# Attention tiles of a transformer block: x loads and h stores on SyncE's queue instead of GpSimd's, and one tile of h transposed by TensorE instead of by DMA

## The chip, the core and the metric

The kernel runs on one core of a Trainium2 chip, in one launch. The metric is the device time in microseconds. The engines are called as in the profile: PE is TensorE (matmuls; PEld its weight loads), DVE is VectorE, ACT is ScalarE, POOL is GpSimd, and SP is SyncE, which computes nothing and issues DMAs. A DMA issued by any of them runs on the core's DMA engines; POOL's go through one queue and SP's through another.

## The reference

Linear attention on a layer-normed x, added to x, and then a gated feed-forward part on the layer-normed sum h. There are 2048 tokens of width 1024, 32 heads of width 32, and F = 3584; all is bfloat16.

```python
def _A_ref(x, wqkv, wo):
    # q, k, v: split of x @ wqkv into 32 heads
    phi = lambda t: jnp.where(t > 0, t + 1, jnp.exp(t)) + 1e-6
    pq, pk = phi(q), phi(k)
    kv = einsum("bhsd,bhse->bhde", pk, v)
    z = einsum("bhsd->bhd", pk)
    num = einsum("bhqd,bhde->bhqe", pq, kv)
    den = einsum("bhqd,bhd->bhq", pq, z)[..., None] + 1e-6
    return heads_joined(num / den) @ wo

def _B_ref(x, W_gate, W_up, W_down):
    gate, up = x @ W_gate, x @ W_up
    return (gate * (gate > 0) * up) @ W_down

h  = x + _A_ref(_layernorm(x), A_wqkv, A_wo)
h2 = h + _B_ref(_layernorm(h), B_W_gate, B_W_up, B_W_down)
```

## The kernel before

The 2048 tokens are 16 tiles of 128. The large products are done by a Strassen-like scheme (`strassen`): seven products of half-size blocks in place of eight, for which sums of the left blocks (`left_sums`, L117 to L120, on DVE) and of the weights are formed first. The matmul accumulates in PSUM tiles with the tags A, D and E; tag D has one buffer.

The program goes through four stages in time. Up to about 125 us, k and v are computed and summed over the tokens (the tiles of x are loaded on SP's queue, normalised, and transposed: the first four by PE in `transpose_in`, L283 and L284, the others by a DMA on SP's queue, L274). Then q is computed, first for one half of the tokens and then for the other. From about 150 to 290 us the attention output and h are made tile by tile, mixed with the second half of q and, later, with the first four f-blocks of the gate and up products (`early_quad`, L705). From about 300 us the rest of the gate and up products (L785) follows, and from about 585 us the down product.

The change is in the third stage. `attn_stages(t)` returns five steps for one tile t, and `attn_step(step)` calls them with a lag of 0, 1, 1, 2 and 4 steps, so that up to five tiles are in work. The list `order` holds the tiles in their order in time; below, "tile n" is the n-th of it, 0 to 15. Tiles 0 to 7 are the first half, whose h the first f-blocks need; the last of it is tile 7, `order[STS - 1]`.

- `nd`: the matmuls of numerator and denominator (L511), their logarithm and exponential on ACT (L515, L517), the quotient on DVE into `o_sb` (L518).
- `oT`: a DMA transpose of `o_sb` into `oT` on SP's queue (L525).
- `x_in`: the tile's x is loaded again for the residual, on POOL's queue (L529), into the buffer `x_res`, of which there are three (`XB`).
- `wo_h`: the matmuls with wo (L541); on DVE the residual addition, which also sums h for the mean (L543, in place in `x_res`); the store of h to DRAM, on POOL's queue (L546); the mean on DVE (L551); on ACT the variance (L553), three small steps (L554 to L556) and the normalised h into the buffer `hn` (L557), of which there are two (`HB`).
- `hn_T`: a DMA transpose of `hn` into its columns of `hnT` on SP's queue (L560).

After `hn_T` of the tiles 4 to 7 and 12 to 15, `attn_step` issues the left sums of that tile's columns on DVE.

An x load reuses the buffer of the tile three before it. It therefore waits until that tile's h is stored and until ACT has read it for the last time (L557). The variance step L553 writes into `hn`, and so waits until the transpose of the tile two before it has landed.

Two other kinds of work share the queues of this stage. The gate and up weights of the first groups are loaded on SP's queue (L486), each held back by a one-element copy on POOL (`hold`, L142) that waits for an `o_sb`. The results of `early_quad` are stored on SP's queue (L720).

The order of the instructions on each engine and queue in this stage isn't written out by hand: it is fixed when the program is built, by the readiness and the priority of each instruction, and the instructions of several steps are interleaved. From the stage of L785 on, PE, DVE and ACT follow the program's order. An engine or queue carries out its list in order, and an instruction that waits holds those behind it.

Of the kernel before, what the change touches and what calls it, by code (L numbers as in the profile page):

```python
# [10 lines left out]
BF16 = mybir.dt.bfloat16  # L11
# [20 lines left out]
def block_kernel(ctx: ExitStack, tc: tile.TileContext, x, wqkv, wo, wg, wu, wd, out, H: int):  # L32
    nc = tc.nc
    P = 128
    xf = x.flatten_outer_dims()
    of = out.flatten_outer_dims()
    S, D = xf.shape
# [4 lines left out]
    KC = D // P  # L42
# [5 lines left out]
    KH = KC // 2  # L48
# [9 lines left out]
    ident = consts.tile([P, P], BF16, name="ident")  # L58
# [12 lines left out]
    h_dram = [[dram.tile([P, NT, D], BF16, name=f"h_dram{i}_{s}") for s in range(NS)] for i in range(2)]  # L71
# [133 lines left out]
    order = [(i * HS + s * SW) // P + tt for s in range(NS) for i in range(2) for tt in range(NT)]  # L205
# [5 lines left out]
    pspool = psctx.enter_context(tc.tile_pool(name="ps", bufs=1, space=PSUM))  # L211
    with ExitStack() as actx:
# [208 lines left out]
        for c in range(KC):  # L421
            bnk, i = divmod(c, GPB)
# [41 lines left out]
    hnT, hns = [], []  # L464
# [32 lines left out]
    def attn_stages(t):  # L497

        i, r = divmod(t * P, HS)
        s, r = divmod(r, SW)  # L500
        st = {}

        def nd():
            o_sb = bwork.tile([P, D], BF16, tag="o_sb", name="o_sb")
            st["o"] = o_sb
            held.append(o_sb)
            ov = o_sb[:].rearrange("p (k h e) -> p k h e", k=KC, h=HPC)
            for c0, n in pieces:
                ps = ndpool.tile([P, NW], FP32, tag="ab", name="nd")
                for c in range(c0, c0 + n):  # L510
                    nc.tensor.matmul(ps[:, (c - c0) * NDW:(c - c0 + 1) * NDW], lhsT=pqT[:, c, t * P:(t + 1) * P],  # L511
                                     rhs=kvz[:, c, :], start=True, stop=True)
                ndv = ps[:, 0:n * NDW].rearrange("p (k w) -> p k w", w=NDW)
                den = bsmall.tile([P, GPB, HPC], FP32, tag="den", name="den")
                nc.scalar.activation(out=den[:, 0:n], in_=ndv[:, :, P:NDW], func=ACT.Ln, bias=deps[:], scale=1.0)  # L515
                rd = bsmall.tile([P, GPB, HPC], FP32, tag="rd", name="rd")
                nc.scalar.activation(out=rd[:, 0:n], in_=den[:, 0:n], func=ACT.Exp, scale=-1.0)  # L517
                nc.vector.tensor_tensor(  # L518
                    out=ov[:, c0:c0 + n], in0=ndv[:, :, 0:P].rearrange("p k (h e) -> p k h e", h=HPC),
                    in1=rd[:, 0:n, :].unsqueeze(3).to_broadcast([P, n, HPC, Dh]), op=ALU.mult)  # L520

        def oT():
            oT = bwork.tile([P, D], BF16, tag="oT", bufs=XB, name="oT")
            st["oT"] = oT[:].rearrange("p (c t) -> p c t", c=KC)
            nc.sync.dma_start_transpose(out=st["oT"], in_=st["o"][:])  # L525

        def x_in():
            x_sb = bwork.tile([P, D], BF16, tag="x_res", bufs=XB, name="x_res")
            nc.gpsimd.dma_start(out=x_sb[:], in_=xf[t * P:(t + 1) * P, :])  # L529
            st["x"] = x_sb  # L530

        def wo_h(borrow):
            h_sb = st["x"]
            tot = bsmall.tile([P, 2], FP32, tag="tot", name="tot")
            for j in range(2):
                if borrow:
                    ps = pspool.tile([P, NW], FP32, tag="E", bufs=2, name="attn")
                else:
                    ps = abpool.tile([P, NW], FP32, tag="ab", name="attn")
                for c in range(KC):  # L540
                    nc.tensor.matmul(ps[:], lhsT=st["oT"][:, c, :], rhs=wo_sb[:, c, j * NW:(j + 1) * NW],  # L541
                                     start=(c == 0), stop=(c == KC - 1))
                nc.vector.scalar_tensor_tensor(out=h_sb[:, j * NW:(j + 1) * NW], in0=ps[:], scalar=1.0,  # L543
                                               in1=h_sb[:, j * NW:(j + 1) * NW], op0=ALU.mult, op1=ALU.add,
                                               accum_out=tot[:, j:j + 1])
            nc.gpsimd.dma_start(out=h_dram[i][s][:, r // P, :], in_=h_sb[:])  # L546
            st["hn"] = bwork.tile([P, D], BF16, tag="hn", bufs=HB, name="hn")

            sm = bsmall.tile([P, 6], FP32, tag="sm", name="sm")
            nmean, var, lnv, rstd, nmr = (sm[:, i:i + 1] for i in range(5))  # L550
            nc.vector.tensor_scalar(out=nmean, in0=tot[:, 0:1], scalar1=tot[:, 1:2], scalar2=-1.0 / D,  # L551
                                    op0=ALU.add, op1=ALU.mult)
            nc.scalar.activation(out=st["hn"][:], in_=h_sb[:], func=ACT.Square, bias=nmean, scale=1.0, accum_out=var)  # L553
            nc.scalar.activation(out=lnv, in_=var, func=ACT.Ln, bias=LN_EPS, scale=1.0 / D)  # L554
            nc.scalar.activation(out=rstd, in_=lnv, func=ACT.Exp, scale=-0.5)
            nc.scalar.activation(out=nmr, in_=nmean, func=ACT.Identity, scale=rstd)  # L556
            nc.scalar.activation(out=st["hn"][:], in_=h_sb[:], func=ACT.Identity, bias=nmr, scale=rstd)  # L557

        def hn_T():
            nc.sync.dma_start_transpose(out=hnT[s][i][:, :, r:r + P], in_=st["hn"][:])  # L560

        return nd, oT, x_in, wo_h, hn_T

    LAG = (0, 1, 1, 2, 4)
    STS = ST // NS
# [163 lines left out]
    for f in range(NE):  # L729
        st = {}  # L730
# [149 lines left out]
    for r, (wt, f, fi, toks) in enumerate(runs):  # L880
        w = [ops() for _, ops in now]
        later = []
        for n, s in enumerate(toks):
# [51 lines left out]
            if k == nwin - 3:  # L935
                for x in range(2):
                    t = wpools[1].tile([P, KC * 2 * GP * P], BF16, tag=("wg", "wu")[x], name="wd")
# [16 lines left out]
    for n in range(2):  # L954
        t = fpool.tile([P, 4 * D], BF16, tag="wraw", bufs=2, name="xd")
# [242 lines left out]
    for n in range(1, len(OUTER)):  # L1198
# [73 lines left out]
        else:  # L1272
            pss = []
            for p in range(4):
# [13 lines left out]
                s, t0 = divmod(2 * p, NT)  # L1288
# [55 lines left out]
```

## Time and profile before

| | |
|---|---|
| median of 3 runs | 750.96 us (750.52 to 752.11) |
| the profiled execution | 750.52 us |
| its span | 748.7 us |
| mean granted PE clock | 0.997 |
| PE busy | 723.2 us, 97% |
| DVE, ACT, POOL busy | 563.1, 322.4, 23.1 us |
| POOL's DMA queue | 32 transfers of 256 KB, 8.39 MB |
| DMA engines, mean rate | 176 GB/s |

The span goes from the first to the last instruction of the profiled execution; the time holds 1.8 us more, of what lies around it. Busy times of several engines overlap. Rows of the timeline show the start in us, the duration in us, the engine, the line and the operation with its output and inputs, the number of instructions merged, and in brackets how long the engine had been idle before and what ended that. Rows of the waits show the total in us, how many times, and the longest. Rows of the stretches show the busy time and number of instructions of PE, PEld, DVE, ACT and POOL, then the granted clock, the busy share of the DMA engines, and GB/s. "SPq" is SP's queue.

### The profile page before, as it was taken

To read this page: it belongs to the slowest core of one execution; us is meant where nothing else is said; L and a number is where in the kernel's file an instruction comes from. 1 tells how busy PE (TensorE), PEld (TensorE's weight loads), DVE (VectorE), ACT (ScalarE), POOL (GpSimd) and SP (SyncE) were. 2 spreads that over 40 slices of the span, in tenths; PEclk is the share of its full clock that TensorE was granted. 3 is DMA by queue.
4 is the path that set the end of the run, shared out by engine and by line. 5 is a ranking of instruction groups with operands and counts; after the bars stand their busy time and mean duration, and the time that the engine had idled before them with its cause. 6 is when DMAs were issued, how large, how long until landed. Compare 5 with 4: busy or idle time off the path is not lost.

```text
span 748.7 us, 10599 instructions
## 1 busy us (share of the span) xinstructions
PE 723.2 (97%) x3967; PEld 382.1 (51%) x4020; DVE 563.1 (75%) x991; ACT 322.4 (43%) x580; POOL 23.1 (3%) x76
## 2 busy tenths in 40 slices
PE   7999999999879989999999999999999999999997
PEld 3444555444434434444444444444444458888666
DVE  6997653775867568687787788877787469996797
ACT  4785653878577555444444344443435220000000
POOL 0000000011111000000000000000000000000000
PEclk9999999999999999999999999999999999999999
DMA  9765003079778635154837439466574299887822
GB/s 319 165 135 155 0 1 111 3 172 222 169 161 185 127 85 180 39 171 126 244 116 204 138 132 313 149 213 221 182 260 148 94 389 360 314 288 297 311 73 83
DMA packets 144532, 132.04 MB, mean 176 GB/s; under 512 B 50912, under 2 KB 128096, under 8 KB 144480
## 3 DMA queue, kind: packets, MB, share of 16 engines
q1 hardware_dynamic: 130784, 114.84, 51.4%
q0 software_dynamic: 2560, 8.39, 3.6%
q10 hardware_dynamic: 11136, 8.13, 3.4%
q8 instruction: 31, 0.51, 0.3%
q14 instruction: 21, 0.17, 0.1%
HBM read 79.95 MB, written 39.85 MB: 160 GB/s over the span
## 4 chain that ended last, share of the span: by engine, by line
PE 77%; DVE 8%; ACT 6%; DMA 6%; issue 2%; SPq 0%; DVEq 0%; POOL 0%; ACTq 0%
PE accA L785 22%; PE accX L785 8%; PE accY L785 8%; PE accA L1117 8%; DMA hn<-hn 3%; PE Aq L298 3%; PE accA L946 3%; PE Aq L438 3%; PE attn L541 3%; PE accX L1117 3%; PE accY L1117 2%; PE Eq L298 2%; PE accY L946 2%; PE accX L946 2%; PE Aq L705 1%
## 5 line engine op out<-in xcount | busy, mean ns | idle before, releaser
L795 ACT ACTIVATE gu<-gu 128x512 bf16<-128x512 bf16 x72 | 45.4, 630 | 131.2 <-DVE gu L794 131.2
L790 ACT COPY snap<-accA 128x1024 f32<-128x1024 f32 x72 | 72.5, 1008 | 36.6 <-PE accA L785 36.5
L541 PE MATMUL attn<-wo_mem,oT 128*128 128x512 bf16 x248 | 59.8, 386 | 5.6 <-DVE x_res L543 3.7
L785 PEld LDWEIGHTS <-tg 128*128 128x128 f16 x384 | 37.5, 98 | 45.3
L785 PEld LDWEIGHTS <-tu 128*128 128x128 f16 x384 | 37.5, 98 | 45.4
L794 DVE TENSOR_TENSOR gu<-accY,snap 128x1024 bf16<-128x1024 f32 x36 | 43.9, 1219 | 10.0 <-ACT snap L790 10.0
L785 PE MATMUL accA<-hn,tg 128*128 128x512 f16 (+1 forms) x192 | 49.3, 379 | 0.0
L785 PE MATMUL accA<-hn,tu 128*128 128x512 f16 (+1 forms) x192 | 49.3, 379 | 0.0
L154 ACT COPY u<-Aq 128x512 f32<-128x512 f32 x56 | 32.3, 582 | 38.5 <-PE Aq L298 20.0
L794 DVE TENSOR_TENSOR gu<-accX,snap 128x1024 bf16<-128x1024 f32 x36 | 43.9, 1219 | 6.5 <-PE accX L785 3.7
L1117 PEld LDWEIGHTS <-x 128*128 128x128 f16 (+1 forms) x448 | 43.8, 98 | 5.6
L785 PEld LDWEIGHTS <-wg 128*128 128x128 bf16 x288 | 28.2, 98 | 34.0
L785 PEld LDWEIGHTS <-wu 128*128 128x128 bf16 x288 | 28.1, 98 | 34.0
L541 PEld LDWEIGHTS <-oT 128*128 128x128 bf16 x256 | 24.9, 99 | 35.0 <-issue 4.9
L798 DVE TENSOR_TENSOR hq<-gu 128x512 bf16<-128x512 bf16 x48 | 20.3, 423 | 14.3 <-ACT gu L795 14.2
L298 PEld LDWEIGHTS <-xT 128*128 128x128 bf16 (+1 forms) x192 | 18.6, 98 | 24.4 <-issue 3.0
L1117 PEld LDWEIGHTS <-xs 128*128 128x128 f16 x280 | 27.3, 98 | 3.4
L543 DVE SCALAR_TENSOR_TENSOR x_res<-attn,x_res 128x512 bf16<-128x512 f32 x32 | 21.9, 687 | 8.6 <-PE attn L541 8.6
L946 PEld LDWEIGHTS <-x 128*128 128x128 bf16 (+1 forms) x168 | 16.4, 98 | 19.6
L518 DVE TENSOR_TENSOR o_sb<-nd,rd 128x384 bf16<-128x384 f32 (+1 forms) x48 | 22.6, 506 | 4.4 <-ACT rd L517 4.4
L1123 DVE TENSOR_TENSOR snap<-accA,u 128x1024 f32<-128x1024 f32 x16 | 19.5, 1219 | 8.4 <-PE accA L1117 8.3
L785 PE MATMUL accA<-hs,tg 128*128 128x512 f16 x96 | 24.6, 379 | 0.0
(234 smaller groups left out, 1418.4 us busy)
## 6 DMA issues: line engine op xcount, KB each, us to landing
x<-x_dram SPq DMA_DIRECT2D x17, 896.0 KB, 8.5
x_dram<-hq SPq DMA_DIRECT2D x28, 512.0 KB, 3.3
wg<-in_B_W_gate_dram SPq DMA_DIRECT2D x14, 512.0 KB, 5.4
wu<-in_B_W_up_dram SPq DMA_DIRECT2D x14, 512.0 KB, 7.2
wraw<-in_B_W_down_dram SPq DMA_DIRECT2D x14, 512.0 KB, 4.9
x_dram<-hq SPq DMA_DIRECT2D x28, 256.0 KB, 2.8
t_dram<-wt SPq DMA_DIRECT2D x28, 256.0 KB, 2.2
xd<-x_dram SPq DMA_DIRECT2D x6, 896.0 KB, 7.0
```

The source lines that it names most:

```text
L154: nc.scalar.copy(out=snaps[nm, v], in_=A[v][:])
L298: nc.tensor.matmul(ps[:], lhsT=left[m - 1][:, kc, r + v * P:r + (v + 1) * P], rhs=right[m - 1][:, kc, :], start=(start and kc == 0), stop= ...
L438: nc.tensor.matmul(ps[:], lhsT=rq[m - 1][:, kc, (c + v) * P:(c + v + 1) * P], rhs=left[m - 1][:, kc, :], start=(start and kc == 0), stop=( ...
L518: nc.vector.tensor_tensor(out=ov[:, c0:c0 + n], in0=ndv[:, :, 0:P].rearrange("p k (h e) -> p k h e", h=HPC), in1=rd[:, 0:n, :].unsqueeze(3 ...
L541: nc.tensor.matmul(ps[:], lhsT=st["oT"][:, c, :], rhs=wo_sb[:, c, j * NW:(j + 1) * NW], start=(c == 0), stop=(c == KC - 1))
L543: nc.vector.scalar_tensor_tensor(out=h_sb[:, j * NW:(j + 1) * NW], in0=ps[:], scalar=1.0, in1=h_sb[:, j * NW:(j + 1) * NW], op0=ALU.mult, ...
L785: nc.tensor.matmul(ps[:, v, :], lhsT=w[v][n - 1][:, kc, :], rhs=left[n - 1][:, kc, :], start=(t is not None and kc == 0), stop=(kc == KH - ...
L790: nc.scalar.copy(out=st[nm][:], in_=halves(st["A"]))
L794: add(out=g[:], in0=halves(st[nm]), in1=st[base][:], op=ALU.add)
L795: nc.scalar.activation(out=g[:, 0, :], in_=g[:, 0, :], func=ACT.Relu)
L946: nc.tensor.matmul(ps[:, t * NW:(t + 1) * NW], lhsT=x_tile(n, s, kh)[:, f, (t0 + t) * P:(t0 + t + 1) * P], rhs=w_tile(n, kh)[:, f, :], sta ...
L1117: nc.tensor.matmul(pv[:, tt, :], lhsT=left(m)[:, f, tt * P:(tt + 1) * P], rhs=right(m)[:, f, :], start=(t is not None and f == 0 and tt % ...
```

## The change

In the attention tiles the x load and the h store are issued by SP instead of POOL. For tile 7, `hn_T` no longer issues a DMA transpose: PE transposes the eight blocks of 128 x 128 into one PSUM tile with the tag D, and ACT and DVE each copy one half of it into `hnT`. The left sums of tile 7 then read it from there as before.

```diff
         def x_in():
             x_sb = bwork.tile([P, D], BF16, tag="x_res", bufs=XB, name="x_res")
-            nc.gpsimd.dma_start(out=x_sb[:], in_=xf[t * P:(t + 1) * P, :])
+            nc.sync.dma_start(out=x_sb[:], in_=xf[t * P:(t + 1) * P, :])
...
-            nc.gpsimd.dma_start(out=h_dram[i][s][:, r // P, :], in_=h_sb[:])
+            nc.sync.dma_start(out=h_dram[i][s][:, r // P, :], in_=h_sb[:])
...
         def hn_T():
+            if t == order[STS - 1]:
+                pt = pspool.tile([P, KC, P], BF16, tag="D", bufs=1, name="tp")
+                for kc in range(KC):
+                    nc.tensor.transpose(pt[:, kc, :], st["hn"][:, kc * P:(kc + 1) * P], ident[:])
+                nc.scalar.copy(out=hnT[s][i][:, 0:KH, r:r + P], in_=pt[:, 0:KH])
+                nc.vector.tensor_copy(out=hnT[s][i][:, KH:KC, r:r + P], in_=pt[:, KH:KC])
+                return
             nc.sync.dma_start_transpose(out=hnT[s][i][:, :, r:r + P], in_=st["hn"][:])
```

## The prediction

> **What bounds the kernel now.** I read the page first, then the chain that ended last, then the stretches of time, the waits and the timeline of the stretch that the change touches. The page says that TensorE (PE) is the bound almost everywhere:
>
> ```profile
> span 748.7 us, 10599 instructions
> PE 723.2 (97%) x3967; PEld 382.1 (51%) x4020; DVE 563.1 (75%) x991; ACT 322.4 (43%) x580; POOL 23.1 (3%) x76
> ```
>
> The stretches show where the missing 25 us lie: from 300 to 585 us PE is busy for 283.81 of 285 us, but from 160 to 230 us for 61.02 of 70, from 230 to 260 for 29.30 of 30, and from 260 to 300 for 36.70 of 40. So the attention stretch, 160 to 300 us, holds 13.0 us of idle PE. What comes after is dense, so that a microsecond won or lost here reaches the end. In the chain that ended last, the transposes of h (`DMA hn<-hn`) have 3.4% of the span: five pieces of 6.14, 6.54, 4.43, 5.42 and 3.06 us. The waits of 150 to 300 us say who stands behind them (total, times, longest):
>
> ```profile
> DVE hs L117 <- DMA hn<-hn: 12.9, 6, 3.8
> ACT hn L553 <- DMA hn<-hn: 4.4, 2, 3.4
> PE attn L541 <- DVE x_res L543: 3.7, 1, 3.7
> PE nd L511 <- DVE o_sb L518: 2.0, 1, 2.0
> ```
>
> PE hardly waits for a transpose itself. VectorE (DVE) does, at the first of the left sums (L117), with the residual additions (L543) queued behind, and those release PE's PSUM tiles. The timeline shows the worst case, tile 5:
>
> ```profile
> 210.00 1.23 SPq L560 DMA_TRANSPOSE hn<-hn  x1
> 210.27 0.54 POOL L529 DMA_DIRECT2D x_res<-in_A_x_dram  x1 [2.35 <-ACT hn L557]
> ...
> 212.26 1.26 SPq L525 DMA_TRANSPOSE oT<-o_sb  x1
> ...
> 216.57 0.42 DVE L117 TENSOR_TENSOR hs<-hn 128x512 f16<-128x512 bf16 x1 [3.79 <-DMA hn<-hn]
> 216.65 1.15 ACT L553 ACTIVATE hn<-x_res,sm 128x1024 bf16<-128x1024 bf16 x1 [3.44 <-DMA hn<-hn]
> ...
> 217.67 0.10 PEld L541 LDWEIGHTS <-oT 128*128 128x128 bf16 x1 [2.57 <-DMA oT<-o_sb]
> ...
> 219.00 1.01 PE L541 MATMUL attn<-wo_mem,oT 128*128 128x512 bf16 x2 [3.71 <-DVE x_res L543]
> ```
>
> One transpose takes 6.5 us and stops DVE, ScalarE (ACT) and PE in turn. After it PE even runs at half clock for 3 us (the granted clock is the 0.50; then share and GB/s of the DMAs):
>
> ```profile
> 219.00:222.00 3.00, 3.00 (x11) 1.41 (x11) 3.00 (x10) 2.60 (x8) 1.08 (x2) 0.50 0.54 49
> ```
>
> That is 1.5 us more, so this stall costs 5.2 us.
>
> **Why the transposes are slow.** I asked for the landing time of each h transpose (L560), and compared it with the nearest x load from GpSimd (POOL, L529). With that load issued between 1.7 us before and 0.9 us after it (tiles 0, 1, 2, 4 to 8, 10, 11, 12) a transpose landed in 6.0, 6.1, 6.0, 5.5, 6.5, 5.6, 4.4, 5.0, 4.5, 4.4 and 5.4 us: median 5.5. Without it (tiles 3, 9, 13, 14, 15) it took 3.1 or 3.3. The pairing is no accident: the load waits for its buffer until the second normalising pass (L557) of the tile three back, which is what releases that tile's transpose. Before 40 us the same 256 KB loads go out on SyncE's (SP's) queue, 0.8 to 1.7 us ahead of a transpose of the same shape (xT), and that one still lands in 3.0 to 3.4 us, once in 4.3. Beside the POOL loads of 40.2 and 49.5 us it takes 4.7 and 6.2.
>
> **Part 1, x loads and h stores from POOL to SP.** POOL loses 32 issues of 0.54 us, none of which anyone waits for. SP gains 32; its own x loads show 0.53 us each, 17 us in all, 29 of them after 160 us. SP is idle for about half of the stretch, so only those that fall in front of a ready transpose count. Load and transpose become ready together, and the load stands first in the program. Load first: the transpose is issued 0.5 us later and has 256 KB ahead of it. A 512 KB weight load issued 0.6 us ahead of an oT transpose (159.2 us) made that one 4.8 us instead of 3.1, so half the bytes cost about 0.85. Sum 0.5 + 0.85 + 3.1 = 4.45 us against the median of 5.5: 1.1 us gained. Transpose first: 3.2 us, 2.3 gained. And if SP's load stretches it as POOL's did, 0.5 lost. I take 1.1, since the rows before 40 us speak against the last.
>
> The Trainium skill, "DMA: Bandwidth & Descriptors", section "Issuing engines are not separate DMA queues", speaks against this: whoever issues, all transfers share the same 16 engines, and spreading them only saves the issuer's time. By it alone the transposes stay as slow, SP's 0.5 us stands in front of each, and the sum of this part is a loss of 1 to 2 us; the split of 5.5 against 3.1 us above is why I don't follow it.
>
> What that pays on PE, by place. Tile 1 (ACT waits 0.93 at 181.7, and PE later 1.3): 0.6. Tile 4 (DVE waits 1.95 at 205, PE 2.0): 1.1 us on DVE, about 0.8 on PE. Tile 5 (PE waits 3.7): what is late next is oT at 217.67, which is 1.3 us before 219.0; a faster oT adds up to 1, and a shorter stall may spare the 1.5 us of half clock: between 0.5 and 4.5, I take 2.0. Tile 12 (DVE waits 3.07 at 261.6, PE 1.67): 1.1. Tiles 13 to 15 have no load beside them: nothing. Sum 4.5.
>
> Against it: the order of SP's queue is fixed, and an h store or x load whose condition comes late holds what stands behind. The compiled order of all engines may shift as well, as instructions here are interleaved by readiness across tiles. No row shows either in the new order: bounds from a gain of 1 to a loss of 4, taken as a loss of 1.5.
>
> **Part 2, tile 7 by TensorE.** Removed: one DMA transpose (221.57, landing at 226.0) and its 1.42 us on SP. Added: eight PE transposes, one ACT copy, one DVE copy. In the first tiles four transposes (L283) start at 11.19 and the next matmul at 11.41, so eight cost PE 0.43 us:
>
> ```profile
> 11.19 0.38 PE L283 MATMUL tp<-ident,xn 128*128 128x128 bf16 x4 [0.17 <-ACT xT L284]
> 11.41 1.03 PE L331 MATMUL kp<-pq_mem,xT 128*128 128x512 bf16 x4
> ```
>
> The copies are those of L284, 0.58 us on ACT and 0.41 on DVE; their cover is that ACT and DVE both wait in this stretch, and without it they cost their length. The "D" tile is free: its last reader ran at 182 us, its next writer starts at 224.8. So tile 7 is ready at about 221.5 instead of 226.0. Gained: PE's wait for L117 at 226.5, 0.66 us, and DVE's 0.77. What is lost depends on the place in PE's order: ahead of the matmuls that resumed at 219.0 they would hold PE until tile 7's h was normalised at 219.99, 1.0 us; behind them nothing. Between a gain of 0.2 and a loss of 0.8 I take a loss of 0.1, and round the part to nothing: what it takes off the DMA engines helps tile 8's transpose, for which nobody waits.
>
> The Trainium skill, "TensorE: Matmul & The Clock Gate", section "Part 4: PE-mode transpose", gives about 275 ns for one transpose in a kernel. Eight would be 2.2 us, and this part an estimated loss of 1.5; the pace of L283 is 54 ns each, and I use that.
>
> **Sum.** 4.5 - 1.5 = 3.0 us gained. The profiled execution took 750.52 us (its span 748.7 and 1.8 around it), so 747.5; the median of the three runs is 0.44 above that execution: 747.9 us.
>
> **Rivals.** *SP's queue becomes the wait* (slower). The x load of tile n also waits until the h store of tile n-3 has landed. Twice that came after the transpose was ready: the store of tile 3 (181.87 + 5.6 = 187.5) against 186.3, that of tile 9 (226.35 + 5.6 = 231.95) against 230.3. With the load ahead of the transpose on SP, this one is 1.2 to 1.6 us late, plus 0.5 of issue: 1.7 to 2.1. Nobody waits for tiles 3 and 9. It decides when it reaches tiles 1, 4, 5 and 12, where the store was ahead by 0.6, 2.6, 2.9 and 2.3 us: stores later by 2 to 3 us are enough. Then four places lose about 1.9 us, two thirds of it on PE (8.6 us of PE idle behind 12.9 on DVE): +5.1, less what shorter landings return, about 1.5: near 754.5 us. Against it: 256 KB stores on SP's queue land in 2.2 and 2.8 us in the page's medians (`t_dram`, `x_dram`), POOL's h stores in 3.5.
>
> *The stalls are handed on* (no change). The DMA engines are 0.88 busy from 160 to 230 us; oT at 217.67 and ACT's chain of 4 us per tile are close behind each stall. Then little remains: 749.5 to 752.4, about 750.7.
>
> *The change doesn't do what it says* is left at no chance: queue and engine are named in each line of the diff.
>
> **How the numbers follow.** Forecast 0.52, own range 743.5 to 749.4; the slower rival 0.33, 752.5 to 756; handed on 0.15. 0.2% is 1.5 us, about what a measurement of this kernel can tell from no change. The range for 8 in 10 reaches from 743.5 (all bounds of part 1 good, with the half clock spared) to 754.5: 743.5 to 754.5. Faster 0.52, same 0.15, slower 0.33.
>
> **What would show it.** Right: h transposes of tiles 4, 5 and 12 landing in under 4.6 us, the sum of `DVE hs L117 <- DMA hn<-hn` falling from 12.9 to below 8, no stretch at clock 0.50 near 220 us, idle PE of 160 to 300 us near 10 us, and PE's L117 wait of tile 7 gone. Wrong: transposes still at 5.5 us with SP loads beside them; SP's queue waiting at L529 or L546 while a transpose is ready; PE waiting for ACT's L557 ahead of the new transposes.

## The result, and the profile after

The changed kernel takes 746.1 us (median of four runs, 745.6 to 746.41), the kernel before 750.74 us (four runs, 750.27 to 752.11): the ratio is 0.9935, 95% interval 0.9917 to 0.9952, so 4.6 us were gained where 3.0 were forecast. The profiled execution took 745.99 us against 750.52.

The page of the changed kernel. POOL has lost its 32 issues, and PE is the bound as before:

```profile
span 744.2 us, 10584 instructions
PE 725.1 (97%) x3974; PEld 383.0 (51%) x4028; DVE 563.4 (76%) x992; ACT 322.7 (43%) x581; POOL 5.7 (1%) x44
```

In the code after the change `hn_T`'s DMA stands on L567 (L560 before), its PE transposes on L563, their two copies on L564 and L565, `early_quad` on L712 (L705 before) and the next stage on L792 (L785 before).

The stretches of the changed kernel, two of the three of the attention stage (the middle one, 230 to 260 us, has 29.31 of 30 us, as before). PE's busy time is the third number:

```profile
160.00:230.00 70.00, 64.18 (x350) 31.28 (x355) 54.64 (x144) 54.41 (x144) 1.01 (x5) 1.00 0.95 203
260.00:300.00 40.00, 38.92 (x177) 17.45 (x179) 28.75 (x68) 22.41 (x42) 0.00 (x0) 1.00 0.47 141
```

Idle PE in 160 to 300 us went from 13.0 to 7.6 us. The clock is 1.00 in both; the 3 us at half clock near 220 us are not there in this execution. It has such a stretch near 10 us instead, long before the attention stage (the 0.50):

```profile
10.00:13.00 3.00, 3.00 (x10) 1.08 (x8) 1.23 (x1) 1.65 (x2) 0.00 (x0) 0.50 1.08 363
```

The waits of the changed kernel, 150 to 300 us (total, times, longest):

```profile
DVE hs L117 <- DMA hn<-hn: 6.0, 6, 3.1
ACT hn L553 <- DMA hn<-hn: 2.3, 2, 1.9
PE Dq L712 <- DVE hn L565: 1.8, 1, 1.8
PE nd L511 <- DVE o_sb L518: 1.0, 2, 0.5
PE tp L563 <- ACT hn L557: 0.9, 1, 0.9
```

DVE's wait for the transposes is halved (12.9 before), ACT's too (4.4), and PE's 3.7 us behind the residual addition are gone. Two waits are new, the third and the fifth, and both come from the transposes on PE.

The worst place of before, tile 5, in the timeline of the changed kernel. The x load is now ahead of the transpose on the same queue, and the transpose, in flight from 208.68 us, has landed at 212.1:

```profile
208.29 0.34 SPq L529 DMA_DIRECT2D x_res<-in_A_x_dram  x1
208.68 1.23 SPq L567 DMA_TRANSPOSE hn<-hn  x1
...
212.13 0.42 DVE L117 TENSOR_TENSOR hs<-hn 128x512 f16<-128x512 bf16 x1 [0.36 <-DMA hn<-hn]
```

And tile 7, a little later in the same timeline, where PE does the transposes:

```profile
215.55 0.23 PE L563 MATMUL tp<-ident,hn 128*128 128x128 bf16 x1 [0.85 <-ACT hn L557]
...
219.07 0.55 PE L563 MATMUL tp<-ident,hn 128*128 128x128 bf16 x7
...
221.53 0.56 ACT L564 COPY hn<-tp 128x512 bf16<-128x512 bf16 x1
...
222.12 0.42 DVE L565 COPY hn<-tp 128x512 bf16<-128x512 bf16 x1
...
222.60 0.81 PE L712 MATMUL Dq<-hn,wg 128*128 128x512 bf16 x3 [1.81 <-DVE hn L565]
```

The first transpose stands in PE's list ahead of 16 matmuls and holds them 0.85 us, until tile 7's h is normalised. After the last, the two copies are queued behind other work of ACT and DVE, and PE's next product into the tag D tile, which the copies still read, waits 1.81 us for them.

**Where the microseconds are.** From the first transpose of `o_sb` to the first matmul of the next stage the kernel before takes 145.82 us (153.32 to 299.14), the changed one 139.48 (154.27 to 293.75): 6.3 us less. Cut into equal pieces from that first transpose, PE's idle time, from the stretches of both profiles, is:

```
us after the first oT   0-50   50-70   70-100   100-120   to the end   sum
before                  1.78    6.60     1.12      2.11         1.43   13.0
after                   1.33    4.49     0.69      0.48         0.60    7.6
part 1 alone (below)    1.26    3.12     0.63      0.72         0.42    6.2
```

5.4 us of the 6.3 are idle time. The rest is PE's busy time, 132.79 before and 131.89 after: about what the half clock, 1.5 us by the prediction's count and absent here, and the 0.78 us of the eight new transposes make together. The last row is the fastest of six runs of part 1 alone; a second profile of it on another chip has 2.0, 3.6, 0.3, 1.2 and 0.5, 7.6 in all. Of the 6.3 us, 0.95 do not arrive, because this execution reached the first transpose of `o_sb` 0.95 us later: the half clock near 10 us lies before it. A second profile of the same kernel, which has none there, reached it at 152.55 us. Another 0.85 us goes behind the stage: from the first matmul of the next stage to the end the kernel before takes 449.6 us, the changed one 450.4 in both its profiles, part 1 alone 449.5 in both. No run shows why.

### The profile page after: what moved, and what is told of

The parts are those of the page before. It is cut to its first block, busy times and chain, and to the rows that moved or that the text cites. A ratio compares the mean times of both kernels' runs of the same rounds, so it can differ in the third digit from the quotient of the medians.

```text
span 744.2 us, 10584 instructions
## 1 busy us (share of the span) xinstructions
PE 725.1 (97%) x3974; PEld 383.0 (51%) x4028; DVE 563.4 (76%) x992; ACT 322.7 (43%) x581; POOL 5.7 (1%) x44
## 4 chain that ended last, share of the span: by engine, by line
PE 70%; DVE 12%; DMA 7%; ACT 7%; issue 3%; SPq 0%; DVEq 0%; POOL 0%; ACTq 0%
PE accA L792 21%; PE accX L792 8%; PE accA L1124 8%; PE accY L792 7%; PE Aq L298 3%; PE accX L1124 3%; PE Aq L438 3%; DMA hn<-hn 2%; PE attn L541 2%; PE accY L1124 2%; PE accA L953 2%; PE Eq L298 2%; ACT hn L553 2%; DVE stats L256 1%; DMA x<-x_dram 1%
## 5 line engine op out<-in xcount | busy, mean ns | idle before, releaser
L792 PEld LDWEIGHTS <-tg 128*128 128x128 f16 x384 | 37.5, 98 | 45.8 <-issue 0.7
L792 PEld LDWEIGHTS <-tu 128*128 128x128 f16 x384 | 37.5, 98 | 45.4
L541 PE MATMUL attn<-wo_mem,oT 128*128 128x512 bf16 x249 | 57.8, 379 | 1.6 <-DMA oT<-o_sb 0.6
L792 PE MATMUL accA<-hn,tg 128*128 128x512 f16 (+1 forms) x192 | 49.3, 379 | 0.2 <-ACT snap L797 0.2
L792 PE MATMUL accA<-hn,tu 128*128 128x512 f16 (+1 forms) x192 | 49.3, 379 | 0.0
L792 PEld LDWEIGHTS <-wg 128*128 128x128 bf16 x288 | 28.1, 98 | 34.0
L792 PEld LDWEIGHTS <-wu 128*128 128x128 bf16 x288 | 28.1, 98 | 34.0
L792 PE MATMUL accA<-hs,tg 128*128 128x512 f16 x96 | 24.6, 379 | 0.0
```

The source lines that it names most:

```text
L792: nc.tensor.matmul(ps[:, v, :], lhsT=w[v][n - 1][:, kc, :], rhs=left[n - 1][:, kc, :], start=(t is not None and kc == 0), stop=(kc == KH - ...
```

## The experiments

They ran on three chips, each with the kernel before beside it (750.09 us on chip A, 751.46 on B, 749.82 on C), and times are compared within a chip or as ratios.

### The two parts by themselves (chip A)

Part 1 alone leaves out the branch in `hn_T`; part 2 alone leaves both DMAs on POOL.

```diff
 # part 1 alone
+            nc.sync.dma_start(out=x_sb[:], in_=xf[t * P:(t + 1) * P, :])
+            nc.sync.dma_start(out=h_dram[i][s][:, r // P, :], in_=h_sb[:])
 # part 2 alone
+            if t == order[STS - 1]:   # PE transposes and two copies, as in the change
```

Expected of part 1 alone:

> Part 1 alone: x loads and h stores on SP, tile 7 still transposed by DMA. Theory of the prediction (a load from POOL stretches the h transpose beside it, the queue is the gain and the PE transpose about nothing): 746 to 747 us, most of the 4.6 us gained; h transposes land in 3.3 to 4.6 us, as in the changed kernel. Rival (the gain comes from taking tile 7's transpose off the DMA engines, with the order it brings): 749.5 to 751, no gain, whatever the transposes do. Second rival (the compiled order): the gain is anywhere, and does not follow the landing times.

Expected of part 2 alone:

> Part 2 alone: tile 7 transposed by PE, x loads and h stores on POOL as before. Theory of the prediction: 749.5 to 751.5 us, within 1 us of before; the h transposes beside a POOL load still land in 4.4 to 6.5 us. Rival (tile 7's DMA transpose is what had to go): 746 to 748.

Measured: part 1 alone 743.93 us (742.28 to 745.1), ratio 0.9919, interval 0.9898 to 0.994, 6.2 us less and below the 746 to 747 us expected; part 2 alone 750.0 us, ratio 1.0009, interval 0.9989 to 1.0028. The waits of part 1 alone:

```profile
DVE hs L117 <- DMA hn<-hn: 5.3, 4, 3.0
ACT hn L553 <- DMA hn<-hn: 2.4, 2, 1.7
PE Eq L705 <- DVE hs L117: 1.3, 1, 1.3
```

and of part 2 alone:

```profile
DVE hs L117 <- DMA hn<-hn: 10.9, 7, 3.5
PE Dq L712 <- DVE hn L565: 1.7, 1, 1.7
```

All of the gain is part 1. Part 2 brings its wait for the copies with it wherever it stands; with part 1 it removes the 1.3 us that PE waits for tile 7's left sum, and puts 1.8 + 0.9 us in their place.

### The changed kernel and part 1 alone, once more (chip B)

> The changed kernel once more, beside part 1 alone on one chip. Theory A (the PE transpose of tile 7 takes back a part of what the queue brings: it holds PE before L557 and the products of tag D behind its copies): 1 to 2 us slower than part 1 alone. Theory B (the PE transpose is worth nothing either way; the earlier difference was between chips): within 0.7 us of part 1 alone.

> Part 1 alone again, as the partner of the three others: 6 us faster than before if the first run was representative, 4.5 us if it was not.

Measured: the changed kernel 744.78 us (743.63 to 745.62), ratio 0.9914, interval 0.9889 to 0.9939; part 1 alone 743.39 us (742.53 to 746.2), ratio 0.9903, interval 0.9876 to 0.9931. The medians differ by 1.4 us in part 1's favour, and the waits add up to as much (1.8 + 0.9 - 1.3), but the intervals overlap: that part 2 gains nothing is shown, that it costs 1.4 us is not. Nor is it clear that the waits account for it: in the two profiles without half clock the attention stage is 0.95 us longer with part 2, and the stages behind it 0.9 us.

The half clock did not go with the stall. This second profile of part 1 alone has it, near the place of before:

```profile
221.00:224.00 3.00, 2.79 (x7) 0.99 (x7) 3.00 (x9) 1.96 (x8) 0.00 (x0) 0.50 0.92 223
```

The mean granted clock of an execution is 0.998 or less in 7 of 12 of part 1 alone, in 8 of 10 of the changed kernel, and in 53 of 62 of the kernel before on the three chips. At 0.999 or more the kernel before takes 747.3 to 748.5 us (9 executions) and part 1 alone 742.3 to 743.4 (5): about 5 us of the gain are there without any half clock.

### The two moves of part 1 by themselves (chip A)

```diff
 # only the x load moves
+            nc.sync.dma_start(out=x_sb[:], in_=xf[t * P:(t + 1) * P, :])
 # only the h store moves
+            nc.sync.dma_start(out=h_dram[i][s][:, r // P, :], in_=h_sb[:])
```

Expected of the x load alone:

> Only the x loads on SP; h stores on POOL, tile 7 by DMA. Theory of the prediction (it is the x load that starts together with the transpose): h transposes land in 3.3 to 4.6 us, nearly the whole gain, 746 to 748 us. Rival (the h stores on POOL stretch them as much, or POOL's queue as a whole does): transposes between 4 and 6 us, half the gain or less, 748 to 750.

Expected of the h store alone:

> Only the h stores on SP; x loads on POOL, tile 7 by DMA. Theory of the prediction: h transposes beside a POOL load still 4.4 to 6.5 us, median above 5; 750 to 751.5 us. Rival (the stores are the disturbance): median of the transposes near 4, 746.5 to 748.5 us.

Measured: the x load alone 744.01 us, ratio 0.992, interval 0.9894 to 0.9946, as much as both moves; the h store alone 751.09 us, ratio 1.0018, interval 1.0002 to 1.0034. The landing times of the h transposes, tile by tile in the order of their issue (us, from the issue; tile 7 has none in the changed kernel):

```
tile            0    1    2    3    4    5    6    7    8    9   10   11   12   13   14   15
before         6.0  6.1  6.0  3.1  5.5  6.5  5.6  4.4  5.0  3.3  4.5  4.4  5.4  3.1  3.1  3.1
changed        3.8  4.6  4.0  3.4  4.1  3.4  5.5   -   4.4  3.5  3.3  3.4  3.5  3.0  3.0  3.2
only x moves   5.4  5.1  4.4  3.3  4.7  3.7  5.7  3.7  5.5  3.5  3.3  3.3  3.4  3.1  3.0  3.0
only h moves   6.7  6.2  4.5  3.0  5.2  6.5  5.4  3.5  4.4  3.1  5.9  7.6  6.1  3.1  3.0  3.0
```

With the x load still on POOL, tiles 10 to 12 take 5.9 to 7.6 us; with only the x load moved, 3.3 to 3.4. At the tiles 0, 1, 4, 6 and 8 the expected 3.3 to 4.6 us did not come with the x load alone (4.7 to 5.7). In the waits, `DVE hs L117 <- DMA hn<-hn` sums to 7.4 us with the x load moved and to 12.9 with the h store moved, the figure of before. The time is in the x loads. PE and ACT carry out the same lists with the x load alone moved as with both moves, and DVE and ACT the same with the h store alone moved as in the kernel before. What this leaves open is how far the new compiled order that comes with the move of the x load has a part in the gain.

The landing times begin at the issue, and they leave out how long a transpose waits on SP's queue before it. From the end of L557, when the normalised h is ready, to the landing it is (us, from the timelines and the landing times; the last row is the kernel of the last experiment):

```
tile            0    1    2    3    4    5    6    7    8    9   10   11   12   13   14   15
before         8.1  6.9  8.2  3.1  5.8  6.6  6.0  6.0  5.2  3.4  4.6  4.4  5.5  3.1  3.1  3.1
changed        7.2  6.5  7.2  4.0  6.8  3.8  6.7   -   5.6  4.9  3.7  3.8  3.9  3.1  3.1  3.2
load behind    5.3  4.9  5.8  3.2  4.9  3.1  4.6  7.0  4.1  3.1  3.1  3.6  3.1  3.1  3.1  3.1
```

Over the ten tiles with a POOL load before and an SP load now (0, 1, 2, 4, 5, 6, 8, 10, 11, 12), the landings are 15.1 us shorter in sum, but the waits before the issue 9.1 us longer. The tiles 0 to 2, 5 and 10 to 12 gain 0.4 to 2.7 us each, 6 and 8 lose 0.7 and 0.4, and tile 4 loses 1.0; still PE's wait of 2.0 us at tile 4 is gone. That is order: before, DVE's list had tile 4's first left sum ahead of the quotients that PE needed,

```profile
205.00 0.42 DVE L117 TENSOR_TENSOR hs<-hn 128x512 f16<-128x512 bf16 x1 [1.95 <-DMA hn<-hn]
...
205.47 1.01 DVE L518 TENSOR_TENSOR o_sb<-nd,rd 128x384 bf16<-128x384 f32 x2
...
206.07 0.34 PE L511 MATMUL nd<-kvz,pq_mem 128*128 128x132 bf16 x3 [1.99 <-DVE o_sb L518]
```

and in the changed kernel it stands behind them:

```profile
203.93 1.01 DVE L518 TENSOR_TENSOR o_sb<-nd,rd 128x384 bf16<-128x384 f32 x2
...
204.53 0.34 PE L511 MATMUL nd<-kvz,pq_mem 128*128 128x132 bf16 x3
...
206.47 0.43 DVE L117 TENSOR_TENSOR hs<-hn 128x512 f16<-128x512 bf16 x1 [0.44 <-DMA hn<-hn]
```

### A load that nobody reads, beside each transpose (chips B and C)

To separate the load's queue from the compiled order and everything else, part 1 alone got an extra load of 256 KB of x into a spare tile, at each h transpose: issued by POOL with one spare tile (chip B), by POOL with two (chip C), and by SP with one (chip C). A one-element copy on POOL makes the load wait until `hn` has been written, as the x load of the kernel before had to.

```diff
         def hn_T():
+            dmy = dpl.tile([P, D], BF16, tag="dmy", name="dmy")   # bufs=1, or 2
+            hold(dmy[0:1, 0:1], st["hn"][0:1, 0:1])
+            nc.gpsimd.dma_start(out=dmy[:], in_=xf[t * P:(t + 1) * P, :])   # or nc.sync
             nc.sync.dma_start_transpose(out=hnT[s][i][:, :, r:r + P], in_=st["hn"][:])
```

POOL, one spare tile:

> Part 1 alone, and POOL again loads 256 KB beside each h transpose: x rows into a spare tile that nobody reads, started when the tile's normalised h is ready. The lists of PE, DVE, ACT and SP are the same as in part 1 alone; only POOL's differs. Theory (a load on POOL's queue stretches the transpose beside it): h transposes back at 4.4 to 6.5 us, the tiles 13 to 15 now too, and 748 to 752 us. Rival (the gain came from the changed order of the instructions, not from the queue): transposes a little slower by the 0.84 us that 256 KB take, 744 to 746 us.

POOL, two spare tiles:

> As the run before with the spare loads on POOL, but with two spare tiles in turn, so that POOL's one-element copy no longer waits for the load before and no longer holds the buffer of the normalised h (ACT waited 4.6 us for it there). The lists of PE, DVE, ACT and SP are again those of part 1 alone. Theory (the spare loads stretch the transposes): tiles 13 to 15 again 4.3 to 4.6 us against 3.0, the others above part 1 alone by 1 us or more, and 749 to 755 us. Rival (the 13 us were the held buffer): 744 to 747 us.

SP, one spare tile:

> Part 1 alone with the same 256 KB spare load beside each h transpose, issued by SP ahead of the transpose. Theory (it is POOL's queue beside SP's that costs; on one queue a load ahead costs little): tiles 13 to 15 land in 3.3 to 3.6 us, 744 to 748 us, clearly below the runs with the spare load on POOL. Rival (256 KB more cost the same wherever they are issued): tiles 13 to 15 at 4.3 us or more, and the same time as with the spare load on POOL.

Measured with one spare tile on POOL: 756.63 us, ratio 1.0073, interval 1.0042 to 1.0103, which is 13.2 us more than part 1 alone on that chip, and beyond the expected 748 to 752. This one can't be read cleanly: ACT waited 4.6 us in two pieces for the copies on POOL, which held the `hn` buffer until a spare tile was free. With two spare tiles that wait is gone: 753.5 us, ratio 1.0049, interval 1.0031 to 1.0068, where part 1 alone had 0.9919 and 0.9903 on the other chips. In both kernels PE, DVE, ACT and SP carry out the same lists as in part 1 alone. The waits of the one with two spare tiles:

```profile
DVE hs L117 <- DMA hn<-hn: 13.1, 8, 4.4
ACT hn L554 <- DMA hn<-hn: 5.4, 3, 2.1
```

Both are at least back at the size of the kernel before (12.9 and 4.4 us). The timeline of the same kernel at tile 13, which has no load beside it in part 1 alone:

```profile
268.40 1.23 SPq L564 DMA_TRANSPOSE hn<-hn  x1
268.44 0.39 POOL L142 COPY dmy<-hn 1x1 bf16<-1x1 bf16 x1 [9.07 <-ACT hn L558]
...
269.12 0.54 POOL L563 DMA_DIRECT2D dmy<-in_A_x_dram  x1 [0.30 <-POOL dmy L142]
```

The load is issued 0.7 us after the transpose, and the transpose lands in 4.5 us; 3.0 in part 1 alone. All sixteen are stretched. Landing times of part 1 alone, from the view of the tile `hn` (least, median, most):

```profile
DMA to landing us min/median/max: 3.0/3.5/5.4
```

and with the spare load on POOL:

```profile
DMA to landing us min/median/max: 4.0/4.5/6.6
```

This also bounds the part of the order. With the same lists, and the transposes of the tiles 4 and 5 back at 5.0 and 4.9 us, PE's gaps at these two tiles (those over 0.25 us) add up to 2.4 us; in part 1 alone they are 0.6, in the kernel before 6.5, with transposes of 5.5 and 6.5 us. So of the 5.9 us gained there about 1.8 follow the transposes. The other 4.1 are the new order or what the transposes of before were longer still; no run separates the two.

Measured with the spare load on SP: 747.07 us, ratio 0.9957, interval 0.9935 to 0.9979: 3 to 4 us more than part 1 alone by the ratios, and 6.4 us less than with the same bytes on POOL, on the same chip. `DVE hs L117 <- DMA hn<-hn` is 7.5 us, and the median landing 4.0 us, behind 512 KB at several tiles (the x load and the spare one). At the tiles 13 to 15 SP issued the spare load behind the transpose (265.43 us after 264.09 at tile 13), and these landed in 3.0 to 3.1 us: at these three tiles a load behind it on the same queue costs a transpose nothing that can be seen. This kernel's lists are not those of part 1 alone, so a part of these 3 to 4 us may be order.

### x loads on ACT's queue (chip C)

```diff
+            nc.scalar.dma_start(out=x_sb[:], in_=xf[t * P:(t + 1) * P, :])   # h stores on SP
```

> Part 1 alone, with the x loads on ACT's hardware queue, a second queue beside SP's but without POOL. Theory 1 (two queues in turn on the same engines stretch the transpose, whoever issues): h transposes of tiles 10 to 12 at 4.3 to 5.5 us as with POOL. Theory 2 (POOL's way of issuing is what costs): 3.3 to 3.6 us as on SP. The time says less, as each issue also takes 0.5 us of ACT, which is in the chain of h: 744 to 752.

Measured: 750.42 us (744.05 to 752.0), ratio 0.9986, interval 0.9962 to 1.0009. The transposes of the tiles 9 to 12, which have an ACT load beside them, land in 3.9, 4.0, 4.1 and 4.7 us: between those beside SP's load (3.3 to 3.6 in part 1 alone) and those beside POOL's (4.4 to 5.4 for tiles 10 to 12 of before). So at these tiles a second queue stretches them also when it is ACT's, though less; the tiles 0 to 6 take 3.1 to 6.4 us. The time says little on its own: PE waited 4.8 us for `oT`, the lists differ, and the first transpose of `o_sb` came at 156.59 us, 3.3 us later than before.

### x loads on POOL, but after the transpose (chip C)

Both DMAs stay on POOL. The x load waits, through a one-element copy on POOL that reads `hnT`, until the transpose of the tile three before it has landed. For that `x_in` is called after `hn_T` within a step.

```diff
-        return nd, oT, x_in, wo_h, hn_T
+        return nd, oT, wo_h, hn_T, x_in
-    LAG = (0, 1, 1, 2, 4)
+    LAG = (0, 1, 2, 4, 1)
...
+            k = order.index(t) - 3
+            if k >= 0:
...
+                hold(x_sb[0:1, 0:1], hnT[s3][i3][0:1, KC - 1, r3:r3 + 1])
             nc.gpsimd.dma_start(out=x_sb[:], in_=xf[t * P:(t + 1) * P, :])
```

> x loads and h stores on POOL as in the kernel before, but an x load starts only when the h transpose of the tile three before has landed (a one-element copy on POOL into the x buffer reads the transposed tile first). Theory (what matters is that the load is not beside the transpose, not who issues it): transposes of tiles 10 to 12 at 3.1 to 3.5 us, 743 to 747 us. Rival (POOL's queue costs by itself, through late x loads or POOL's own waits): 749 us or more.

Measured: 746.75 us, ratio 0.9946, interval 0.9927 to 0.9965: 3.1 us gained with not one DMA taken from POOL. The tiles 10 to 12 land in 3.4, 3.0 and 3.0 us. Where a load that was held for one tile starts beside the transpose of another, that one is stretched: POOL loads at 180.38 us (an h store follows it at 180.91) and 211.43 us, 0.2 and 0.9 us after the transposes of the tiles 2 and 6, which take 6.8 and 7.4 us. Why it gains less than part 1 stands in its waits:

```profile
DVE hs L117 <- DMA hn<-hn: 4.8, 5, 3.0
DVE x_res L548 <- DMA x_res<-in_A_x_dram: 4.4, 1, 4.4
PE attn L546 <- DVE x_res L548: 3.9, 1, 3.9
```

DVE hardly waits for transposes any more, but once for an x load that now comes late, and PE behind it.

### The load behind the transpose on SP's queue (chip B)

Part 1 alone, with `x_in` called after `hn_T` in a step, by the new `return` and `LAG` of the diff above.

> Part 1 alone, with the x load called after the transpose of h in each step instead of before it, so that SP issues the transpose first. Prediction's bound (the x load ahead costs 0.5 us of issue and some transfer): h transposes land in 3.1 to 3.3 us and are issued 0.4 to 0.5 us earlier, 742 to 744 us, 0.5 to 1.5 us faster than part 1 alone. Rival (transposes are no longer what PE waits for, or the load now comes late): within 0.7 us of part 1 alone or slower.

Measured: 741.88 us (741.51 to 743.81), ratio 0.988, interval 0.9853 to 0.9908: the lowest median of all, 9.6 us under the kernel before on that chip and 2.9 us under the changed one (743.63 to 745.62 there). The intervals of these two ratios overlap slightly, and that of part 1 alone more, so that its lead over part 1 alone is not shown. Its median transpose lands in 3.1 us, against 3.5 with the load ahead. Its lists differ from those of part 1 alone. From the ready h to the landing it has the shortest times of the table above at nearly all tiles, as a transpose no longer waits behind the x load.

## Why the prediction was right, and where its sizes were off

**What bounds the stage** held: 13.0 us of idle PE between 160 and 300 us, and what was won there reached the end. It ended at 7.6 us where about 10 were named. Of the signs named for right all came in the changed kernel: the tiles 4, 5 and 12 land in 4.1, 3.4 and 3.5 us (under 4.6), DVE's wait is 6.0 (under 8), PE's wait at L117 for tile 7 is gone, and there is no half clock near 220 us. The first was counted from the issue, though, and by the ready h tile 4 is no earlier; the last can't be put down to the change, as part 1 alone has the half clock again in one of its two profiles. Of those named for wrong two came too: SP waiting at L529 once, and PE waiting for L557 ahead of its transposes.

**The cause of the slow transposes** held, and is now shown rather than paired, though not that the whole gain comes from it: the same load on POOL, with the lists of four engines unchanged, stretches every transpose and makes the kernel about 10 us slower than without it; held back until the transpose is done, it leaves them at 3.0 to 3.4 us at the tiles 10 to 12, where nothing else starts beside them. The pairing in the trace of before (5.5 against 3.1 us) was not a common third cause such as the crowded stretch; that stretch adds to it, since tile 6 still takes 5.5 us with the load on SP.

**The rule of the Trainium skill** that was weighed, "DMA: Bandwidth & Descriptors", "Issuing engines are not separate DMA queues", would have made part 1 a loss of 1 to 2 us. The measurement decides against that reading: it gained 6.2. That all queues run on the same engines doesn't contradict this, but what a transfer costs its neighbour depended on the queue it came from.

**Landing with the load ahead on SP.** The working had 0.85 us for the bytes and 3.1 for the transpose, 3.95 in all. Over the ten tiles that had a POOL load before and have an SP load now, the median is 3.9 (5.55 before). At the calm tiles 10 to 12 it is 3.3 to 3.5, so the bytes cost 0.2 to 0.4 us there; at tiles 1 and 6 it is 4.6 and 5.5. The 0.5 us for the wait behind the load was too little: at the ten tiles the wait before the issue grew by 0.4 to 2.3 us, 0.9 on average. From the ready h to the landing 1.1 us was to be gained at each, and 0.6 on average came.

**Places on PE**, from the table of idle time, for part 1 alone. Tile 1: 0.6 was taken, 0.5 came in the first profile, nothing in the second. Tiles 4 and 5: 0.8 + 2.0 taken; 3.5 us of idle time went in the first profile, where the half clock went as well, and 3.0 in the second, where it stayed. The 0.8 of tile 4 came by luck: its transpose was no earlier, and DVE's new order did it. Tile 12: 1.1 taken, 1.4 and 0.9 came. Between these places and behind tile 12 nothing was taken, and 1.5 and 1.7 came. In all 6.9 and 5.4 us of idle time went where 4.5 were taken; what was too small is thus mostly the places that were put at nothing.

**The loss of 1.5 for SP's order** is the other wrong size: PE did not show it. The queue did hold the transposes longer, by the 9.1 us above, and the order of the other engines changed too, but to PE's advantage. 4.5 - 1.5 = 3.0 for part 1 should have been about 6.

**Part 2 as nothing** was wrong in its working, if not much in its sum. The hold at L557 was foreseen as 0 to 1.0 us and was 0.85. The D tile was called free, its last reader long done and its next writer due at 224.8 us. But PE itself came sooner, and its next writer was ready at 220.8 us (222.60 less the wait of 1.81), while ACT and DVE had yet to copy the transposes out. That they "both wait in this stretch" was no cover: the copies were queued behind other work and ended 2.9 us after the last transpose (219.62 to 222.54). Gained against that: the wait at L117, 1.3 us with part 1 in place. The eight transposes took 0.23 + 0.55 = 0.78 us on PE; 0.43 was taken. The skill's 275 ns each ("TensorE: Matmul & The Clock Gate", "Part 4: PE-mode transpose") would make 2.2 us; this row says 98 ns each.

**The rivals.** An x load that held SP's queue for an h store came once, at the place that the working names first: the x load of tile 6, issued at 187.02 us ahead of tile 3's transpose at 187.41, waited 2.0 us for tile 3's h store (1.2 was worked out, without the issue). The waits of SP in the changed kernel, 150 to 300 us:

```profile
SPq L529 <- DMA h_dram<-x_res: 2.0, 1, 2.0
```

It is the only one for a store, and between 186 and 196 us no engine waits for an h transpose: as put down, nobody needed tile 3 yet. It never reached the tiles 1, 4, 5 and 12; the h stores land on SP in 3.4 us in the median, on POOL in 3.5, and were not later by the 2 to 3 us that this rival needed. What did hold tile 4's transpose, for 2.65 us after its h was ready, were a weight load, the x load and a transpose of `o_sb` ahead of it in the list. Stalls handed on: a little of it did, in the changed kernel as the two waits of part 2, and most plainly where x loads were delayed on POOL (3.9 us of PE for a late load). The forecast of 747.9 us lies 1.8 us above the median measured: part 1 was put about 3 us too small, part 2 about 1.4 us too good by the medians, and the two errors partly cancel.

**Still open.** Why a load on another queue stretches a transpose by more than its bytes. The Trainium skill, "DMA: Bandwidth & Descriptors", "Queues, rings and completion order", says that a DMA engine takes packets in turn from the queues that have work for it; that would let a load on its own queue cut into a transpose already begun, while one on the same queue waits behind it, as the 3.0 to 3.1 us of the spare SP load at the tiles 13 to 15 suggest. No run here shows the order of the packets. Open too is how the 6 us of part 1 divide between the shorter transposes and the order; how much of the load-last version's lead, and of the 3 to 4 us of the spare SP load, is order as well; and how the gain of the kernel where POOL waits for the transpose, whose order also differs from before, divides between the two.

## What to carry to other kernels

When a short DMA transfer on whose landing an engine waits takes longer at some places than at others, list its landing times beside every transfer that another queue starts within a microsecond or two, and put the one that is not urgent on the same queue, behind or just ahead of the urgent one. For a step that goes to an idle-looking engine, look not only at who used its PSUM tile last but at who writes it next, and at where the copies that free it stand in their engines' lists. Count such a landing from the moment when its input is ready, and not from its issue, or the wait on the queue drops out. When a stretch at lower clock stands behind a stall, look at more than one execution before it is counted as won.

## What the runs showed of the hardware

A load of 256 KB on POOL's queue beside a transpose of 128x1024 on SP's made that land in 4.0 to 4.5 us instead of 3.0 in the calm tiles 13 to 15, and in 5.9 to 7.6 us at the tiles 10 to 12 with only the h stores moved; the longest of all, 9.5 us, is tile 8 with the spare load on POOL and one spare tile. By the page of before, POOL's queue as a whole held the DMA engines for 3.6% of 748.7 us in 32 transfers, 0.84 us each, less than most of these stretches. On SP's queue the loads themselves were quicker too: the median x load landed in 3.1 us after the change, in 4.5 before. So were the transposes of `o_sb`, which the prediction leaves aside: 3.3 us in the median, 5.0 before.

The length of one wait does not decide whether a stretch at half clock follows. A wait of 3.71 us on PE was followed by one in the kernel before and one of 2.05 us in the version with the load behind the transpose, but one of 2.89 us in the kernel with two spare tiles (273.33 us) by none. The clock records of the fourteen traces have a simple pattern: the stretches inside the program last 3.41 us each and begin a whole number of 3.41 us after the first record (63 of them in the kernel before, where it lasts from 218.91 to 222.32 us). Cut into pieces on that grid, all 24 pieces in which PE was idle for 2.05 us or more were followed by one at half clock, and none with 1.94 us or less was; of two with 2.00 us one was. The wait of 2.89 us lay across two pieces, 0.89 in one and 2.00 in the other. So the same idle time can cost a half clock in one execution and not in the next, as it falls on the grid.
